# A 1-core attention-and-convolution kernel: x transposed by the DMA crossbar instead of TensorE

## The chip, the cores and the metric

The kernel runs on one core of a Trainium2 chip. The metric is device time in microseconds (us), the median of several executions. Each profile is one execution. Its span is about 1.8 us shorter than that execution's time (931.7 against 933.56 for the kernel before).

Ratios are the mean time of one kernel's fast runs over that of the other's fast runs of the same rounds, with a 95% interval. They are not quite the ratios of the medians quoted beside them.

In the profile lines PE is TensorE, PEld its weight loads, DVE VectorE, ACT ScalarE, POOL GpSimd and SP the engine of the sync queue; a q behind the name is the engine's sequencer, which also issues DMAs. L955 is line 955 of that kernel, x970 a count, `a<-b` an output and what it is made from, ps the memory that TensorE writes its results to. In a costs line the numbers are busy us, mean ns of one, and idle us just before, with what ended most of it. In a line in order of time the bracket is the idle time before it and what ended it.

## The reference, cut to what matters

```python
x = A_q                                          # [1, 2048, 640] bf16
g = sigmoid((x * gate_w).sum(-1, keepdims=True))
a = A_ref(x, A_k, A_v, ...)                      # shifted k times v, long convolution by FFT, times x
b = B_ref(x, wq, wk, wv, wo)                     # attention, 32 heads of 20, one shared k and v head
return g * a + (1 - g) * b
```

x is needed in two layouts: transposed (the 640 columns on partitions) as an operand of the q, k, v and gate projections at the start, and as it is for the gating near the end.

## The kernel before

The program builds a graph of operations and deals them to the engines with a list scheduler of its own. The scheduler walks a model clock, using a cost written at each operation, and fixes every engine's order before the kernel is built. When it finds TensorE under-used it inserts filler matmuls on zeros, to keep TensorE's clock up. A changed cost anywhere can therefore deal the whole attention anew. I call one such order a "deal", and the time before the first exponential the "head".

```python
def loads(self):
    ...
    self.dma(T["gw5"][:, :], ..., writes=["gw5"], nbytes=2000, prio=-6.5)
    self.dma(T["wqst"][:, :, 0:160], wq[:, :, 0:160], ..., prio=-5.5)
    for b in range(NB):                       # 4 blocks of 512 rows
        xl = self.dma(T["xn"][:, 4*b:4*b+4, :], x[:, 4*b:4*b+4, :], writes=[("xn", b)], nbytes=655360, prio=-8 + b)

def xT(self):
    for b in range(NB):
        for dc in range(NDC):                 # 5 column blocks of 128
            gr = self.group("xT", ...)
            for ci in range(4):
                self.mm(gr, lambda e, bk, ...: e.transpose(self.bank_bf(bk, 128, 128*ci), T["xn"][...], T["ident"][:, :]), ...)
            al = self.copy_alts(out, lambda bk: self.bank_bf(bk, 512), True)     # VectorE or ScalarE, as dealt
            self.evac(gr, "dve", None, (), [("xT", b)], 0.45, alts=al)
...                                           # then: query projection, key projection of block 0, key/value
...                                           # projection (kvn), largest key norm, key projections of blocks 1 to 3
def EXP(u, h):
    op("act", lambda e, ...: e.activation(T[f"ET{slot}"][:, :], self.ps[...], ACT.Exp, scale=SCALE), ..., 0.91, name="exp", ...)
...
sch.filler0 = lambda e: e.matmul(self.bank(6)..., self.T["zeros"][:, :], idn, start=True, stop=True)   # fillers of the head
```

## Time and profile before

| what | value |
|---|---|
| time, median | 933.17 us (3 runs), 933.53 with the run beside the changed kernel |
| ScalarE busy | 908.2 us, 97% of the span |
| first exponential starts | 27.67 us |
| from there to the end | 904.0 us |
| idle of ScalarE ahead of the later exponentials | 3.9 us in 7 waits |
| TensorE busy, mean granted clock | 86%, 0.985 |

The page is read from its chain, which is nearly all exponentials on ScalarE. The question is then what precedes the first one and what holds up the others. The prediction shows the lines for both.

### The profile page before, as it was taken

How to read it: one execution, taken by the hardware profiler on the slowest of the kernel's cores; microseconds unless marked ns; L12 is line 12 of the kernel's file. 1: busy time of each engine (PE TensorE's matmuls, PEld its weight loads, DVE VectorE, ACT ScalarE, POOL GpSimd, SP SyncE). 2: the span in 40 equal slices, each digit the busy share in tenths (PEclk: the TensorE clock that was granted, in tenths of full speed). 3: DMA queues.
4: the chain of work that ended last, by engine and by line, in shares of the span. 5: the costliest groups of instructions: out<-in, count | busy, mean ns of one | idle time of the engine just before them, and what ended most of it. 6: DMA issues, size and time to landing. Idle time of an engine off the chain costs nothing.

```text
span 931.7 us, 16366 instructions
## 1 busy us (share of the span) xinstructions
PE 798.1 (86%) x6849; PEld 336.6 (36%) x6913; DVE 617.1 (66%) x816; ACT 908.2 (97%) x1003; POOL 385.8 (41%) x331
## 2 busy tenths in 40 slices
PE   7777778988899888999988899889998889987885
PEld 4222213433444334443332344334443424332132
DVE  7666884466775876676677586567667666566364
ACT  7899999999999999999999999999999999999996
POOL 2870002787423368344285253668354860000000
PEclk9999999999999999999999999999999989999799
DMA  5422632001000001000000100000000012111000
GB/s 158 170 76 79 204 121 64 13 7 40 19 19 19 19 2 41 19 18 19 19 28 16 54 19 18 16 16 7 19 18 19 13 36 74 56 50 42 13 13 29
DMA packets 32631, 39.23 MB, mean 42 GB/s; under 512 B 12371, under 2 KB 25805, under 8 KB 32557
## 3 DMA queue, kind: packets, MB, share of 16 engines
q1 hardware_dynamic: 30957, 37.80, 12.8%
q8 instruction: 54, 0.88, 0.4%
q10 hardware_dynamic: 1600, 0.38, 0.2%
q14 instruction: 20, 0.16, 0.1%
HBM read 31.76 MB, written 6.02 MB: 41 GB/s over the span
## 4 chain that ended last, share of the span: by engine, by line
ACT 94%; PE 5%; DVE 0%; issue 0%; DVEq 0%; POOL 0%; POOLq 0%
ACT ET L955 93%; PE ps L939 1%; PE ps L1387 1%; PE ps L981 1%; ACT xT L545 1%; PE ps L1237 0%; PE ps L1391 0%; PE ps L825 0%; PE ps L839 0%; PE ps L1099 0%; ACT Tsin L734 0%; ACT Tcos L737 0%; DVE outsb L1121 0%; PE ps L1106 0%; ACT L741 0%
## 5 line engine op out<-in xcount | busy, mean ns | idle before, releaser
L955 ACT ACTIVATE ET<-ps 128x1024 bf16<-128x1024 f32 x970 | 890.7, 1196 | 7.0 <-PE ps L939 6.7
L939 PE MATMUL ps<-qT,kT 21*128 21x512 bf16 x2048 | 225.0, 389 | 109.6 <-ACT ET L955 101.4
L1268 POOL TENSOR_TENSOR Pp<-X,K 128x512 f32<-128x512 bf16 x120 | 163.7, 1390 | 269.2 <-DVE K L1256 269.1
L981 PE MATMUL ps<-ET,vaug 128*32 128x512 bf16 x1940 | 209.6, 394 | 1.0 <-ACT ET L955 1.0
L939 PEld LDWEIGHTS ps<-qT,kT 21*128 21x128 bf16 x2048 | 56.2, 91 | 275.4 <-ACT ET L955 266.5
L981 PEld LDWEIGHTS ps<-ET,vaug 128*32 128x32 bf16 x1940 | 52.3, 93 | 117.8 <-issue 113.9
L969 DVE TENSOR_SCALAR dJ<-ps 128x1024 uint32<-128x1024 f32 x54 | 66.0, 1222 | 40.1 <-PE ps L939 39.6
L1268 POOL TENSOR_TENSOR AB<-Pp 128x256 bf16<-128x256 f32 x80 | 82.9, 1036 | 6.1
L974 DVE SCALAR_TENSOR_TENSOR dE<-dJ,dE 128x1024 f32<-128x1024 uint16 x54 | 78.2, 1447 | 0.5
L1301 PE MATMUL ps<-AB,Tcos 128*128 128x256 bf16 x320 | 76.0, 275 | 0.8 <-DVE K L1256 0.7
L977 DVE SCALAR_TENSOR_TENSOR ETd<-dJ,dE 128x1024 bf16<-128x1024 f32 x54 | 75.4, 1397 | 0.8
L976 DVE SCALAR_TENSOR_TENSOR dJ<-dJ 128x1024 f32<-128x1024 uint16 x54 | 73.4, 1359 | 0.7
L1301 PE MATMUL ps<-AB,Tsin 128*128 128x256 bf16 x280 | 67.4, 274 | 0.0
L1387 PE MATMUL ps<-Tcos,zeros 128*128 128x512 bf16 x181 | 60.4, 409 | 5.5 <-issue 5.4
L1268 POOL TENSOR_TENSOR Pp<-Pp 128x512 f32<-128x512 f32 x40 | 59.4, 1486 | 3.1
L1039 DVE COPY acc<-ps 128x512 f32<-128x512 f32 x31 | 21.4, 691 | 49.7 <-PE ps L981 49.3
L1237 PE MATMUL ps<-kv,Tcos 128*128 128x256 bf16 x320 | 47.7, 278 | 1.4 <-DVE K L1256 1.0
L1248 DVE TENSOR_SCALAR X<-ps 128x512 bf16<-128x512 f32 x35 | 24.2, 690 | 37.0 <-PE ps L1237 36.5
L1254 DVE CAST K<-ps 128x256 bf16<-128x256 f32 x40 | 16.9, 423 | 47.5 <-PE ps L1237 47.4
L1237 PE MATMUL ps<-kv,Tsin 128*128 128x256 bf16 x320 | 48.2, 275 | 0.0
L1237 PE MATMUL ps<-ssm_kT,Tsin 128*128 128x256 bf16 x320 | 47.8, 274 | 0.0
L1237 PE MATMUL ps<-ssm_kT,Tcos 128*128 128x256 bf16 x320 | 46.0, 275 | 1.0 <-DVE X L1248 0.5
(137 smaller groups left out, 785.6 us busy)
## 6 DMA issues: line engine op xcount, KB each, us to landing
kslab<-in_A_k_dram SPq DMA_DIRECT2D x15, 640.0 KB, 3.4
rbc<-scr_d SPq DMA_DIRECT2D x31, 256.0 KB
scr_o<-oTn SPq DMA_DIRECT2D x24, 128.0 KB, 1.7
xn<-in_A_q_dram SPq DMA_DIRECT2D x4, 640.0 KB
vslab<-in_A_v_dram SPq DMA_DIRECT2D x16, 160.0 KB, 2.9
kst<-in_A_ssm_k_dram SPq DMA_DIRECT2D x5, 512.0 KB
out_dram<-outsb SPq DMA_DIRECT2D x14, 160.0 KB, 1.8
oTp<-scr_o SPq DMA_DIRECT2D x12, 160.0 KB
```

The costliest lines, as they stand in the source:

```text
L939: o = op("pe", lambda e, r=r, Iu=Iu, g=g, j=j, bk=banks[r]: e.matmul(self.bank(bk), T["kT4"][32 * r:32 * r + 21, 128 * j:128 * j + 128], T ...
L955: op("act", lambda e, p=p, slot=slot: e.activation(T[f"ET{slot}"][:, :], self.ps[:, 1024 * p:1024 * p + 1024], ACT.Exp, scale=SCALE), [("p ...
L969: V(lambda e, p=p: e.tensor_scalar(J[:, :], self.ps[:, 1024 * p:1024 * p + 1024], SCALE * LOG2E * 65536.0, EOFF * 65536.0, ALU.mult, ALU.add),
L974: V(lambda e: e.scalar_tensor_tensor(Ef, lo, ED, Ef, ALU.add, ALU.mult), [kJ, "dE"], ["dE"], c_ps(1024), **k)
L976: V(lambda e: e.scalar_tensor_tensor(Jf, lo, EP, lo, ALU.add, ALU.mult), [kJ], [kJ], c_ps(1024), **k)
L977: V(lambda e: e.scalar_tensor_tensor(T["ETd"][:, :], Jf, EQ, Ef, ALU.add, ALU.mult), [kJ, "dE"], ["ETd"], c_ps(1024), **k)
L981: return op("pe", lambda e, r=r, j=j, src=src: e.matmul(self.bank(6)[32 * r:32 * r + 32, :], T["vaug"][:, j, :], src[:, 512 * (r % 2):512 ...
L1237: o = self.mm(gr, lambda e, bk, lhs=lhs, rhs=rhs, comp=comp, n=n: e.matmul(self.bank(bk, 256, 256 * comp), lhs, rhs, start=(n == 0), stop= ...
L1248: self.evac(gr, "dve", lambda e, bk, parts=parts: e.tensor_scalar(X[:, :, :, :].rearrange("p i a c -> p a i c"), self.bank(bk).rearrange(" ...
L1268: f = lambda e: e.tensor_tensor(out, a, b, alu)
L1301: self.mm(gr, lambda e, bk, lhs=lhs, fc=fc, comp=comp, h=h: e.matmul(self.bank(bk, 256, 256 * h), lhs, AB[:, fc, :, comp, :], start=(fc == ...
L1387: sch.filler = lambda e: e.matmul(self.bank(6), self.T["zeros"][:, :], self.T["Tcos"][:, 0, 0:512], start=False, stop=False)
```

## The change

The intent is to take the transposes off TensorE and their evacuations off ScalarE and VectorE: the DMA writes x already transposed. The plain x is loaded after the first query row, since only the gating reads it. The two small weight loads move to ScalarE's DMA queue, which leaves the sync queue to the transposes.

```diff
-                 nbytes=50000, eng="act", prio=-99)          # wk, wv
+                 nbytes=50000, eng="act", prio=-98.8)        # and -98.7
-        self.dma(T["gw5"]..., prio=-6.5)
-        self.dma(T["wqst"][:, :, 0:160], ..., prio=-5.5)
+        self.dma(T["gw5"]..., eng="act", prio=-98.5)
+        self.dma(T["wqst"][:, :, 0:160], ..., eng="act", prio=-98.9)
         for b in range(NB):
-            xl = self.dma(T["xn"][:, 4 * b:4 * b + 4, :], x[...], writes=[("xn", b)], nbytes=655360, prio=-8 + b)
+            o = T["xT"][:, :, 512 * b:512 * b + 512]
+            i = aps["A_q"][0][512 * b:512 * b + 512, :]
+            xl = self.g.add("sp", lambda e, o=o, i=i: e.dma_start_transpose(o, i), (), [("xT", b)], 0.1, kind="d",
+                            nbytes=1000000, prio=-8 + b)
...
-    def xT(self):                                            # the whole function goes
+    def load_x(self):
+        for b in range(NB):
+            self.dma(T["xn"][:, 4 * b:4 * b + 4, :], x[...], writes=[("xn", b)], nbytes=655360,
+                     prio=30 + b, name="ld_x", after=self.crow0)
...
-                [("ps", 2 * p), ("ps", 2 * p + 1)], [("ET", slot)], 0.91, name="exp", main=True,
+                [("ps", 2 * p), ("ps", 2 * p + 1)], [("ET", slot)], 0.904, name="exp", main=True,
```

The last hunk is not about x: it changes the scheduled cost of an exponential.

More of the change, by code (lines that the diff above doesn't have):

```diff
@@ L656, in loads @@
         self.dma(T["wkv"][:, :, 0:20], aps["B_wk"].rearrange("(dc p) c -> p dc c", p=128), writes=["wk"],
-                 nbytes=50000, eng="act", prio=-99)
+                 nbytes=50000, eng="act", prio=-98.8)
         self.dma(T["wkv"][:, :, 20:40], aps["B_wv"].rearrange("(dc p) c -> p dc c", p=128), writes=["wv"],
-                 nbytes=50000, eng="act", prio=-99)
+                 nbytes=50000, eng="act", prio=-98.7)
         wq = aps["B_wq"].rearrange("(dc p) n -> p dc n", p=128)
         self.dma(T["gw5"][:, :], aps["gate_w"].rearrange("(dc p) -> dc p", p=128), writes=["gw5"], nbytes=2000,
-                 prio=-6.5)
-        self.dma(T["wqst"][:, :, 0:160], wq[:, :, 0:160], writes=[("wqst", 0)], nbytes=204800, prio=-5.5)
+                 eng="act", prio=-98.5)
+        self.dma(T["wqst"][:, :, 0:160], wq[:, :, 0:160], writes=[("wqst", 0)], nbytes=204800, eng="act", prio=-98.9)
         xl = None
         for b in range(NB):
-            xl = self.dma(T["xn"][:, 4 * b:4 * b + 4, :], x[:, 4 * b:4 * b + 4, :], writes=[("xn", b)], nbytes=655360,
-                          prio=-8 + b)
+            o = T["xT"][:, :, 512 * b:512 * b + 512]
+            i = aps["A_q"][0][512 * b:512 * b + 512, :]
+            xl = self.g.add("sp", lambda e, o=o, i=i: e.dma_start_transpose(o, i), (), [("xT", b)], 0.1, kind="d",
+                            nbytes=1000000, prio=-8 + b)
         self.xl = [xl]
@@ L797, in weights2 @@
                       [("wqst", 1)], [("wq_pad", 1)], 1.5, prio=-4, name="wq_cp")
-    def xT(self):
+    def load_x(self):
         T = self.T
+        x = self.aps["A_q"][0].rearrange("(i p) d -> p i d", p=128)
         for b in range(NB):
-            for dc in range(NDC):
-                gr = self.group("xT", 1.0 + 0.1 * b, banks=(0, 1, 2, 3, 4, 5, 7))
-                for ci in range(4):
-                    i = 4 * b + ci
-                    self.mm(gr, lambda e, bk, i=i, dc=dc, ci=ci: e.transpose(
-                        self.bank_bf(bk, 128, 128 * ci), T["xn"][:, i, 128 * dc:128 * dc + 128], T["ident"][:, :]),
-                        [("xn", b), "ident"], 0.1)
-                out = T["xT"][:, dc, 512 * b:512 * b + 512]
-                al = self.copy_alts(out, lambda bk: self.bank_bf(bk, 512), True)
-                self.evac(gr, "dve", None, (), [("xT", b)], 0.45, alts=al)
+            self.dma(T["xn"][:, 4 * b:4 * b + 4, :], x[:, 4 * b:4 * b + 4, :], writes=[("xn", b)], nbytes=655360,
+                     prio=30 + b, name="ld_x", after=self.crow0)
     def kproj(self):
@@ L1361, in build @@
         self.weights()
-        self.xT()
         self.kproj()
@@ L1369, in build @@
         self.tables2()
+        self.load_x()
         self.g.fence(["kslab", "vslab", "w4", "kprod", "kshs"], ["iota_f", "iota_s", "tprod", "tcosp"])
```

## The prediction

> **What bounds the kernel now.** I read the page's chain that ended last first, then the chain in order of time, then the order-of-time view of ScalarE and TensorE in the first 28 us, then the waits of ScalarE. The chain by line:
>
> ```profile
> ACT 94%; PE 5%; DVE 0%; issue 0%; DVEq 0%; POOL 0%; POOLq 0%
> L955 ACT ACTIVATE ET<-ps 128x1024 bf16<-128x1024 f32 x970 | 890.7, 1196 | 7.0 <-PE ps L939 6.7
> ```
>
> The reader is to see that ScalarE carries 94% of the end-setting path, nearly all of it the 970 exponentials of the attention, and that it sat idle ahead of them for only 7.0 us. The change touches none of the 970. What it can move is what lies before the first of them. The same path in order of time, first microseconds:
>
> ```profile
> 2.97 3.59 PE ps L1391 x8
> 6.56 0.93 PE ps L806 x12
> ...
> 8.23 0.97 ACT xT L545 x2
> ...
> 16.22 0.61 ACT xT L545
> ...
> 18.60 0.66 PE ps L839 x20
> 19.26 0.53 PE ps L897 x2
> 19.79 2.16 PE ps L839 x60
> ...
> 23.14 3.19 PE ps L825 x14
> 26.33 0.89 issue
> 27.22 0.45 PE ps L939 x4
> 27.67 75.26 ACT ET L955 x82
> ```
>
> (Columns: start us, length us, what.) The first exponential starts at 27.67 us. Before it the path runs through the x transposes on TensorE (L806), their evacuations on ScalarE (xT, L545), the key/value projection (L839), the key-norm maximum and the key projection (L825). After it, the tail of the kernel: the last exponential ends at 922.6 and 9.1 us of output projection and store follow; the change leaves those as they are. So the head of 27.67 us, 3% of the span, is the whole stake, and 2% of 933.17 is 18.7 us, two thirds of that head.
>
> The tile view of xT gives the evacuations:
>
> ```profile
> L545 ACT ACTIVATE xT<-ps x14: 587/597/627, 7.0 to 19.9; 128x512 bf16<-128x512 bf16 x14
> L544 DVE COPY xT<-ps x6: 415/424/425, 11.9 to 18.1; 128x512 bf16<-128x512 bf16 x6
> ```
>
> (Durations are min/median/max ns, then first and last start.) The last x block is usable only when the evacuations near 20 us have ended, although x itself had landed long before: the stretches of 2 us show 214, 345, 306, 321 and 245 GB/s from 2 to 12 us, together 2.86 MB, which is x (2.62 MB) and the small weights; then 40 GB/s. x was on chip at about 11.5 us. The 8 us between are the price of the TensorE path.
>
> **What the Trainium skill says.** "VectorE: DVE Perf Modes", section "The three transpose paths", gives 128x128 bf16 as 390 ns on TensorE and 1309 ns by the DMA crossbar. The trace has a TensorE transpose at a median of 219 ns, but 24 of them fill 1.79 us, 75 ns each when pipelined; so the page's figure is a latency, and I take its 1309 ns with the same doubt. "Advanced Engine Details and Errata", section "X-Bar Transpose (TRN2)", calls transposing DMAs as fast as regular ones, 350 to 400 GB/s; "DMA: Bandwidth & Descriptors", section "Latency and other measured facts", gives 261 GB/s for one kernel with a non-contiguous middle dimension, and this case writes such a layout (five column blocks of a row go to five places of a partition). No run of the kernel before shows a transposing DMA. The same section of the Advanced page wants no second transpose stream in flight; here all four come from one queue.
>
> **The change, part by part.**
>
> *Removed:* 80 transposes, 80 x 75 ns = 6.0 us of TensorE; 14 evacuations on ScalarE (chained starts about 0.48 to 0.61 us apart, some 7.5 us) and 6 on VectorE (6 x 0.42 = 2.5 us). Of these ScalarE's are on the path, interleaved with eight sine tables that stay.
>
> *Added:* four transposing DMAs of 655 KB on the sync queue, 2.62 MB. At 261 GB/s that is 10.0 us, and with the start of about 2 us that the plain loads show (issue at 0.73, flow from about 2) the last block would land at about 13 us with the small loads beside it. The program's author counts each as 1,000,000 bytes in place of 655,360, a belief in about two thirds of the plain rate; applied to the 320 GB/s that the plain loads show, this is 209 GB/s, 12.5 us, landing at about 15. I choose 16 us as my central estimate of the last landing, a little later, as any work per tile on the issuing side can only add.
>
> *Moved:* the first query weights and the gate weights go to ScalarE's queue: two more issues of about 0.5 us ahead of its table load. These are before its first sine, which VectorE's products hold back anyway; ScalarE then has some 10 us of slack. The later load of x as it is (2.62 MB) follows the first key slabs after 27 us, when the DMA engines have room (page: 2 to 6 tenths busy in the 23 us slices up to 160 us), and is used only from the convolution on. I count nothing for it.
>
> *New order on TensorE* (the built kernel's instruction order shows it): 18 filler matmuls, 10 query-projection, 6 filler, 5 key projection, 6 filler, 2 norms, one gate transpose, 80 key/value, 6 filler, then the maximum and 15 key projections as before. Fillers are fixed work in program order, so TensorE has a floor that no fast DMA goes under: start 2.97; the first 8 fillers 3.59 (as before), 10 more at the 0.216 us spacing that the projections show = 2.2, so 8.7; 10 query 2.2, so 10.9; 6 fillers 1.3, 12.2; 5 key 1.1, 13.3; 6 fillers 1.3, 14.6; norms 0.5, gate transpose and its copy about 0.5, 15.6; 80 key/value 2.2, so **17.8 us**. In the kernel before, this point (end of L839) is at 21.95. From there to the first exponential the order is unchanged and took 27.67 - 21.95 = 5.7 us. So the first exponential comes at about 23.5, 4.2 us earlier, if the last block lands before about 17.2 (its own 20 key/value matmuls need 0.6 us). For each us that it lands later, the exponential is a us later; break-even is a landing at 21.3 us.
>
> *The attention:* the scheduled cost of an exponential is changed from 0.91 to 0.904, which reshuffles fillers and side work. Idle of ScalarE in that stage was 3.9 us in 7 waits (the waits of ScalarE after 30 us), so it can give at most about 4 us back; a reshuffle can also cost 1 or 2. I count zero, with a spread of 2.
>
> Sum: -4.2 with a landing at 16 us. I shade it to -4 because a late first block can leave TensorE idle and start it below its pace: 933.17 - 4.2 = about **929.0 us**.
>
> **Rivals.**
>
> *The DMA becomes the new wait.* If a transposing transfer runs well below the plain one, the last landing, not TensorE's order, sets the head. At 136 GB/s (2.62 MB over 19.3 us) it lands at 21.3 and the change is worth nothing; at 100 GB/s it lands at about 28 and costs 7 us, 940; at the 1309 ns per tile of the skill's table taken as serial, 80 tiles take 105 us and the first exponential is at some 113 us, an end near 1018. For it: a row's block of 128 columns is 256 bytes, so x falls into 10,240 such pieces, far smaller than the 1,280-byte rows of the plain load. Against it: two pages with figures of 261 and more, and the queue's order, which puts nothing ahead of the four transfers.
>
> *ScalarE or VectorE holds the head anyway.* The eight sines and two table loads stay on ScalarE, the 16 table products on VectorE. For it: in the kernel before ScalarE is busy without a gap from 7.5 to 21.5. Against: the gap-free stretch holds 7.5 us of the copies that go; what stays would end near 13 us, before TensorE's 17.8. Were it to bind, the gain would shrink to 1 or 2 us: 931.5.
>
> *Hidden anyway / given back later.* The head shortens by 4 us, but the exponentials are then held by something whose time is not tied to the head, such as the slower start of k and v loads behind the added load of x. Against: the ScalarE queue has only 3.9 us of idle over 895 us, so nothing but the exponentials' own length paces it. It would make 931 to 934.
>
> **Range and chances.** Central case (landing by 17 us, weight 0.55): 926.5 to 931. Landing between 17 and 21 (0.2): 929 to 933. Between 21 and 30 (0.15): 933 to 942. Later (0.1): above 942, and about 0.06 above the 951.8 that is 2% slower. Faster by 2% would need the first exponential at 9 us, which TensorE's fillers and projections alone forbid. I choose 923.5 to 937 as the range: it leaves about 0.05 below (a lucky reshuffle added) and 0.15 above.
>
> **What would show it.** In the changed kernel: no matmul of line L806's kind and no evacuation into xT; the four transposes landing at about 16 us and DMA throughput of 200 GB/s or more up to there; the end of the key/value matmuls near 17.8 us; the first exponential near 23.5; the idle ahead of the exponentials and their mean unchanged; and the time from the first exponential to the end still about 904 us. The prediction is wrong if the key/value matmuls wait for the transpose (the first or the last block), or if the part after the first exponential moves by more than 2 us.

## The result, and the profile after

The changed kernel took 928.96 us (median of 4, 928.4 to 931.0) against 933.53 us. The ratio is 0.9957, interval [0.9934, 0.998]: about 4 us, within 2%. The chain and the exponentials of the changed kernel:

```profile
ACT 93%; PE 5%; DVE 0%; issue 0%; DVEq 0%; POOL 0%; POOLq 0%
L950 ACT ACTIVATE ET<-ps 128x1024 bf16<-128x1024 f32 x970 | 890.6, 1198 | 5.7 <-PE ps L934 5.1
```

The 970 exponentials take the same busy time, 890.6 against 890.7 us, so the bound is the same. The chain of the head in order of time (start us, length us, what):

```profile
2.96 5.47 PE ps L1386 x18
8.43 2.16 PE ps L876 x10
10.59 1.29 PE ps L1386 x6
11.89 1.08 PE ps L820 x5
12.97 1.29 PE ps L1386 x6
14.26 0.58 PE ps L892 x2
...
14.87 0.68 DVE ci L898
15.55 0.10 DVE wkv L815
...
15.69 0.89 PE ps L834 x29
...
17.48 0.67 PE ps L834 x20
18.15 1.30 PE ps L1386 x6
...
23.87 0.45 PE ps L934 x4
24.33 21.18 ACT ET L950 x23
```

There is no evacuation of x left, and no DMA in this chain: it is TensorE's own program order (fillers, query projection, fillers, key projection, fillers, norms), a short detour over VectorE, then the key/value matmuls. The first exponential comes at 24.33 us in place of 27.67. The sync queue of the changed kernel in order of time:

```profile
0.73 13.20 SPq L668 DMA_TRANSPOSE xT<-in_A_q_dram  x4
16.07 0.42 SPq L511 DMA_DIRECT2D wqst<-in_B_wq_dram  x1
```

The issue at 16.07 waits for the last transpose, so the last block had landed by then. Its 20 key/value matmuls start at 17.48, so the DMA had 1.4 us to spare. The waits of ScalarE after the first exponential, first the kernel before, then the changed one (total us, times, longest):

```profile
ACT ET L955 <- PE ps L939: 3.9, 7, 1.2
```

```profile
ACT ET L950 <- PE ps L934: 2.4, 5, 0.7
```

From the first exponential to the end: 904.0 us before, 902.7 after. So 3.35 us of the profiles' difference lie ahead of the first exponential and 1.35 us behind it. The experiments ask two things: what sets the head now, and whether the 1.35 us belong to the change.

### The profile page after: what moved, and what is told of

Read it like the earlier page. It is cut to its first block, busy times and chain, and to the rows that moved or that the text cites. A ratio compares the mean times of both kernels' runs of the same rounds, so it can differ in the third digit from the quotient of the medians.

```text
span 927.0 us, 16240 instructions
## 1 busy us (share of the span) xinstructions
PE 802.8 (87%) x6829; PEld 332.5 (36%) x6829; DVE 607.5 (66%) x810; ACT 901.0 (97%) x989; POOL 377.9 (41%) x331
## 4 chain that ended last, share of the span: by engine, by line
ACT 93%; PE 5%; DVE 0%; issue 0%; DVEq 0%; POOL 0%; POOLq 0%
ACT ET L950 93%; PE ps L1386 1%; PE ps L934 1%; PE ps L1382 1%; PE ps L976 1%; PE ps L820 0%; PE ps L1232 0%; PE ps L1094 0%; PE ps L876 0%; PE ps L1296 0%; PE ps L1178 0%; DVE outsb L1116 0%; PE ps L1101 0%; PE ps L834 0%; DVEq L445 0%
## 5 line engine op out<-in xcount | busy, mean ns | idle before, releaser
L950 ACT ACTIVATE ET<-ps 128x1024 bf16<-128x1024 f32 x970 | 890.6, 1198 | 5.7 <-PE ps L934 5.1
L969 DVE SCALAR_TENSOR_TENSOR dE<-dJ,dE 128x1024 f32<-128x1024 uint16 x54 | 75.5, 1399 | 0.6
L971 DVE SCALAR_TENSOR_TENSOR dJ<-dJ 128x1024 f32<-128x1024 uint16 x54 | 71.2, 1318 | 0.6
L1382 PE MATMUL ps<-Tcos,zeros 128*128 128x512 bf16 x207 | 67.0, 403 | 0.0
L1232 PE MATMUL ps<-ssm_kT,Tsin 128*128 128x256 bf16 x320 | 50.4, 274 | 0.0
L967 DVE TENSOR_SCALAR dE<-dJ 128x1024 uint32<-128x1024 uint32 x54 | 45.6, 845 | 1.4
L876 PE MATMUL ps<-xT,wq_pad 128*128 128x512 bf16 x160 | 44.0, 382 | 1.9 <-DVE qT L544 1.1
```

The costliest lines, as they stand in the source:

```text
L950: op("act", lambda e, p=p, slot=slot: e.activation(T[f"ET{slot}"][:, :], self.ps[:, 1024 * p:1024 * p + 1024], ACT.Exp, scale=SCALE), [("p ...
L967: V(lambda e: e.tensor_scalar(E[:, :], J[:, :], 7, 0x7F800000, ALU.logical_shift_left, ALU.bitwise_and), [kJ], ["dE"], c_fast(1024), **k)
L969: V(lambda e: e.scalar_tensor_tensor(Ef, lo, ED, Ef, ALU.add, ALU.mult), [kJ, "dE"], ["dE"], c_ps(1024), **k)
L971: V(lambda e: e.scalar_tensor_tensor(Jf, lo, EP, lo, ALU.add, ALU.mult), [kJ], [kJ], c_ps(1024), **k)
L1232: o = self.mm(gr, lambda e, bk, lhs=lhs, rhs=rhs, comp=comp, n=n: e.matmul(self.bank(bk, 256, 256 * comp), lhs, rhs, start=(n == 0), stop= ...
L1382: sch.filler = lambda e: e.matmul(self.bank(6), self.T["zeros"][:, :], self.T["Tcos"][:, 0, 0:512], start=False, stop=False)
```

## The experiments

In these tables, "rest" is span minus start of the first exponential, "idle" is ScalarE's later waits for TensorE, both from one profile each.

Together on one chip (kernel before 935.09 us):

| run | first exp. | rest | idle | time | ratio |
|---|---|---|---|---|---|
| after_910 | 25.96 | 908.1 | 7.0 | 933.66 | 0.9976 [0.995, 1.0002] |
| before_904 | 28.13 | 905.6 | 4.6 | 934.02 | 0.9984 [0.9958, 1.001] |
| before_moves | 30.19 | 905.3 | 4.9 | 938.84 | 1.0037 [1.0013, 1.0061] |
| fill_first | 28.23 | 901.9 | 1.4 | 930.19 | 0.9948 [0.9926, 0.9969] |

On another chip (kernel before 935.6 us):

| run | first exp. | rest | idle | time | ratio |
|---|---|---|---|---|---|
| two_more | 30.61 | 903.5 | 2.9 | 935.75 | 1.0005 [0.9986, 1.0023] |
| fill_none | 24.80 | 901.9 | 2.4 | 929.48 | 0.9938 [0.9919, 0.9957] |
| x_beside | 31.98 | 900.7 | 1.4 | 934.22 | 0.9997 [0.9969, 1.0026] |
| after_again | 24.97 | 903.4 | 3.0 | 928.95 | 0.9927 [0.9909, 0.9945] |
| after_910_again | 24.50 | 905.5 | 5.0 | 934.32 | 0.9987 [0.9968, 1.0007] |
| after_907 | 24.57 | 903.1 | 3.2 | 929.96 | 0.9945 [0.993, 0.996] |
| head_mended | 24.53 | 902.7 | 1.6 | 928.72 | 0.9929 [0.9912, 0.9946] |

Rest minus idle lies between 899.3 and 901.1 us in all of them, whatever the head: the rest is, within 2 us, a constant plus what ScalarE waits.

### Two more transposes ahead: does the head count one for one?

```diff
             def tr(e, o=o, i=i, b=b):
+                if b == 0:
+                    for n in range(2):       # into the space of the plain x, overwritten later
+                        e.dma_start_transpose(xo_n, x_block_n).then_inc(self.xsem, 16)
                 return e.dma_start_transpose(o, i)
```

The order of all engines is as in the changed kernel.

> The changed kernel, same schedule, with two more transposing transfers of the same size ahead of the four (into space that is overwritten later). Theory (1.4 us of slack behind the landing at 16.07, after that one us late for one us; each transfer takes the 3.29 us of its issue): landing at about 22.6, first exponential at 22.6 + 0.6 + 0.5 + 5.7 = 29.4 us, so 5 us later than in the changed kernel and 934 us, ratio 1.001. Rival (the landing is hidden by other work of the head, as in a head bound by the tables or the fillers): first exponential 24.3 to 26 us, 929 to 931.

The first exponential came at 30.61 us, 5.6 us after that of after_again, and the time rose by 6.8 us on the same chip with the same deal. So the head counts at about one for one here; the rest is unchanged (903.5 against 903.4). In x_beside, below, it counts for less: 7.0 us later and 5.3 us slower than after_again. The road was not the one expected. All blocks had landed by 21.3 us, before TensorE's order reached the key/value matmuls at 21.99. It had waited for the first block instead:

```profile
12.95 3.95 PE L886 MATMUL ps<-xT,wq_pad 128*128 128x512 bf16 x10 [4.42 <-DMA xT<-in_A_q_dram]
```

The ten query projections stood idle 4.42 us for the first block and then took 3.95 us in place of 2.32, because TensorE's clock had fallen meanwhile (granted clock 0.50 from 14 to 16 us). In an in-order program an early first block can matter more than an early last one.

### Fillers taken out: is TensorE's order the bound?

```diff
+        drop = set(o for r in runs[1:] for o in r)      # fill_none: all runs of the head; fill_first: all but the first
+        sch.order["pe"] = [o for o in pe if o not in drop]
```

> The changed kernel, same schedule, with three of the four runs of filler matmuls in the head taken out (6 each; the first 18 stay). Theory (the head is now TensorE's own order, with the transposes' landing at 16.07 us 1.4 us behind it): the key/value matmuls catch up with the last transposed block, the last key square starts at 17.2 in place of 18.62, the first exponential comes at about 22.9 in place of 24.3, and the time falls by about 1.4 us, ratio 0.994. Rival 1 (the landing of the transposes already sets the head): nothing moves, 24.3. Rival 2 (TensorE runs slower without the fillers): matmuls of 128x512 take more than the 0.216 us spacing and the gain is lost.

> The changed kernel, same schedule, with all fillers of the head taken out. Theory (transposes' landing is the next bound): first exponential at about 22.9 us, as with three of the four runs out; the last transposed block at 16.07 sets it. Rival (fillers hold TensorE at speed): the first ten projections take about 0.45 us each, as the first eight fillers of the kernel before did, and the first exponential is at 23.5 or later.

My theory failed in both: I expected 22.9 us, and got 28.23 and 24.80. In fill_none (order of time on TensorE):

```profile
7.51 4.03 PE L876 MATMUL ps<-xT,wq_pad 128*128 128x512 bf16 x10 [7.51 <-DMA xT<-in_A_q_dram]
11.37 1.24 PE L820 MATMUL ps<-xT,wk 128*128 128x512 bf16 x5
14.72 0.59 PE L892 MATMUL ps<-sq,IndG 128*8 128x512 bf16 x2 [2.11 <-DVE IndG L709]
15.25 0.17 PE L813 MATMUL ps<-ident,gw 5*128 5x5 bf16 x1
16.18 2.46 PE L834 MATMUL ps<-wkv,xT 128*128 128x41 bf16 x80 [0.75 <-DVE wkv L815]
```

The first block lands at 7.51 us, so the projections can start 0.9 us sooner, but at half speed (4.03 us for ten; the clock column does not show this first stretch, the durations do). Then the norms wait 2.11 us for small constant columns that VectorE makes late in its order. The fillers filled waits that exist anyway. The bound of the head is thus the program order of TensorE together with VectorE's small operations, and removing fillers alone gains nothing: 929.48 against 928.95 us.

fill_first shows what a gap can cost. After the same 2.11 us wait the granted clock fell to 0.50 and stayed there up to 26 us (length of the stretch, TensorE busy, clock, DMA share, GB/s):

```profile
14.00:16.00 2.00, 0.56 (x2) 0.94 0.64 144
16.00:18.00 2.00, 1.26 (x30) 0.50 0.44 82
...
24.00:26.00 2.00, 2.00 (x6) 0.50 0.40 108
```

In fill_none the same wait was followed by no fall: its clock is 1.00 in every stretch from 14 to 28 us. So a gap of this length may cost the clock or not, and these runs do not show what decides. In fill_first's profile the first exponential is 3.9 us later than in the first profile of the changed kernel. Yet the median, 930.19, does not lie that far from the kernels with all fillers, so one execution's head is not every execution's.

### The plain x loaded beside the transposes: what holds the transposes?

```diff
+            for b in range(NB):              # on the scalar queue, right after the gate weights
+                e.dma_start(T["xn"][:, 4*b:4*b+4, :], x[:, 4*b:4*b+4, :]).then_inc(self.xsem, 16)
```

> The changed kernel, same schedule, with a second, plain load of x (2.62 MB) issued on the scalar queue at the start, beside the transposes. Theory (the transposes are held by their own issue on the sync queue, 3.29 us each, while the DMA engines are half busy): the four issues still take about 3.3 us each, the last lands at 16 to 18 us. Rival (the transposes are held by the DMA engines): two streams share, issues stretch to 5 us or more and the last lands at 21 us or later, the first exponential at 28 us. In both cases scalar work starts about 2 us later, which has 2.6 us of room.

The rival's forecast of the landing came true. The tile view of xT, first the changed kernel, then this one (min/median/max ns of an issue, first and last start us):

```profile
L668 SPq DMA_TRANSPOSE xT<-in_A_q_dram x4: 3157/3287/3330, 0.7 to 10.6; - x4
```

```profile
L674 SPq DMA_TRANSPOSE xT<-in_A_q_dram x4: 3013/3859/7605, 0.7 to 16.0; - x4
```

One of the four issues stretched to 7.6 us and the last block arrived at about 23.6 us. The first exponential came at 31.98, 4 us later than the rival said: the landing was 2.6 us later than its 21, and TensorE's clock fell to 0.50 while it waited 4.11 us for that block. I had taken a DMA figure near 1.1 in a 2 us stretch for half busy, but it is the mean busy share of all 16 engines. Compare the kernel before (plain loads), the changed one (transposes) and this run (both):

```profile
4.00:6.00 2.00, 2.00 (x6) 0.66 (x5) 2.00 (x7) 0.73 (x1) 0.36 (x2) 1.00 1.13 345
```

```profile
4.00:6.00 2.00, 2.00 (x6) 0.70 (x5) 2.00 (x5) 1.99 (x5) 1.13 (x2) 1.00 1.34 228
```

```profile
12.00:14.00 2.00, 2.00 (x11) 0.87 (x9) 1.64 (x8) 1.98 (x3) 0.00 (x0) 1.00 1.11 371
20.00:22.00 2.00, 0.00 (x0) 0.00 (x0) 0.55 (x3) 0.03 (x1) 0.00 (x0) 0.58 1.20 74
```

(Length of the stretch; busy us of TensorE, its weight loads, VectorE, ScalarE and GpSimd; then clock, DMA share, GB/s.) By this share the engines look full at 228 GB/s with transposes and at 345 GB/s with plain loads. But a full share is no fixed limit of bytes: with both streams they moved 371 GB/s at a share of 1.11, and only 74 at 1.20. So the two streams hold each other up, which my theory excluded; whether it is the engines themselves or something else on the transposing path is not shown. The plain x is better loaded after the transposes than beside them, where it costs the whole gain (ratio 0.9997).

### The weight loads alone

```diff
-        self.dma(T["gw5"]..., prio=-6.5)
+        self.dma(T["gw5"]..., eng="act", prio=-98.5)       # and the first query weights, in the kernel before
```

> The kernel before with only the first query weights and the gate weights moved to the scalar queue, ahead of x. Theory (the evacuations of the transposes hold the head, not the weights): first exponential within 1 us of 27.7 us, ratio 0.999 to 1.001. Rival (the weights' wait of 3.1 us on GpSimd was the head's limit and most of the gain comes from the move): first exponential near 25 us, ratio 0.997.

It was slower than both theories allowed: first exponential at 30.19 us, ratio 1.0037. GpSimd copied the query weights at 6.24 us in place of 10.33 (it still waited 2.68 us for them, in place of 3.09), but four issues on ScalarE's queue delayed its table load, from 1.87 to 4.47 us. The first evacuation of x starts only 0.25 us later, at 7.27 us, yet the one that the query projections wait for starts at 13.38 in place of 11.87: the head was dealt anew as well, and how much of this the table load causes is not shown. TensorE's query projections began at 14.04 in place of 12.78 us and ran at half speed (granted clock 0.53 from 14 to 16 us), 634 ns a matmul in the median in place of 379:

```profile
6.24 0.85 POOL L786 COPY wq_pad<-wqst 128x800 bf16<-128x800 bf16 x1 [2.68 <-DMA wqst<-in_B_wq_dram]
14.04 4.02 PE L881 MATMUL ps<-xT,wq_pad 128*128 128x512 bf16 x10 [0.77 <-ACT xT L545]
```

The moved loads are no gain by themselves. Whether they help in the order without evacuations was not tested: no run has the changed kernel without them.

### The scheduled cost of an exponential

```diff
-        0.904, name="exp"      # after_910, after_907: the changed kernel with 0.91 or 0.907
-        0.91, name="exp"       # before_904: the kernel before with 0.904
```

> The changed kernel with the scheduled cost of an exponential put back from 0.904 to 0.91; the instruction order of the head is the same, that of the attention is dealt anew. Theory (the gain is the earlier first exponential, 3.35 us in the profiles; the 1.35 us gained after it is an accident of the deal): first exponential at 24.3 us, and 0 to 2 us slower than the changed kernel, so 929 to 931. Rival (the new cost is a real part of the gain): the stretch after the first exponential is back at 904 us and the ratio to the kernel before is nearer 1, about 0.9965 in place of 0.9957.

> The kernel before with only the scheduled cost of an exponential changed to 0.904. Theory (accident of the deal): ratio to the kernel before between 0.998 and 1.002, with no fixed sign, first exponential at 27.7 us. Rival (the cost is worth 1.3 us by itself): ratio 0.9985, and the idle ahead of the exponentials falls from 3.9 to about 2.4 us.

> The changed kernel with the scheduled cost at 0.91, second time. If the deal of the attention is worth something: slower than the changed kernel of the same call by 1.5 to 4 us, with idle ahead of the exponentials again near 7 us in place of 2 to 3. If the earlier 7.0 was one execution's accident (dips of the granted clock): the same time as the changed kernel within 1 us, idle between 2 and 5 us.

> The changed kernel with the scheduled cost at 0.907, half way: a third deal with the same head. If the time followed the cost, it would lie between 0.904 and 0.91. If it is an accident of each deal, it lies anywhere within 4 us of either, with its idle as the measure: time minus that of the changed kernel equals the difference of the two idle sums.

> The changed kernel again, unaltered, for a comparison with the two next runs on one chip. Ratio to the kernel before 0.9957 within its interval; first exponential between 24.3 and 26.0 us by the length of TensorE's half-speed start (5.5 to 6.9 us for the first 18 fillers in the profiles so far); idle ahead of the exponentials after the first 2 to 3 us.

My theory of after_910 (929 to 931 us) failed: it took 933.66 us. With one chip and the same head in program order, 0.904, 0.907 and 0.91 gave 928.95, 929.96 and 934.32 us. The changed kernel without its new cost is only 0.1 to 0.2% faster than the kernel before (ratios 0.9976 and 0.9987, 1 within both intervals). The kernel before with the new cost is not clearly faster (0.9984, interval around 1), and its idle rose from 3.9 to 4.6 us. So the cost isn't worth something by itself: it picks a deal, and the deals of the changed kernel differ by up to 5 us. The idle of one profile does not account for that by itself: after_910_again idles 2.0 us more than after_again and its median is 5.4 us longer, and after_907 idles 0.2 more and is 1.0 longer. The profiled execution of after_910_again, 932.95, was one of its faster ones.

What a deal does is seen at 867 to 873 us. First the kernel before, then the changed one with 0.91 (from 870), then the changed one (columns as above):

```profile
867.00:870.00 3.00, 2.01 (x11) 0.43 (x11) 1.92 (x3) 2.77 (x4) 0.00 (x0) 0.52 0.03 3
870.00:873.00 3.00, 2.53 (x15) 0.66 (x15) 2.96 (x4) 2.09 (x3) 0.00 (x0) 0.50 0.03 3
```

```profile
870.00:873.00 3.00, 3.00 (x16) 0.53 (x12) 2.43 (x4) 2.47 (x3) 0.00 (x0) 0.50 0.03 3
```

```profile
867.00:870.00 3.00, 2.22 (x15) 0.50 (x11) 2.93 (x5) 3.00 (x5) 0.00 (x0) 1.00 0.18 56
870.00:873.00 3.00, 2.42 (x21) 0.64 (x21) 1.84 (x2) 3.00 (x5) 0.00 (x0) 1.00 0.16 56
```

In the first two TensorE's clock has fallen to one half and ScalarE waits for scores (2.09 and 2.47 busy of 3). In the third neither happens. Both profiles with 0.91 in the changed kernel, and both of the kernel before, have waits near 763 and 870 us; both profiles of the changed kernel have waits near 772 and 779 and none near 870. The places recur with the deal. One place does not make a deal slow: after_907 falls at 863 us too and is nearly as fast as after_again. Others, such as one near 487 us in the kernel before, appear in one execution and not in the next.

> The kernel before again, unaltered, for a second profile of it. Theory (the changed kernel gains from an earlier first exponential and from a deal with fewer falls of TensorE's clock): first exponential at 27.7 to 28.2 us, the stretch after it 904 to 907 us, idle ahead of the exponentials 4 to 7 us with waits again near 526, 760 and 870 us. Rival (the first profile's 3.9 us was typical and the clock falls are random): idle 2 to 4 us at other places. Ratio to itself 1.000 within its interval.

The kernel before a second time: 934.81 us, ratio to itself 0.9995 [0.9954, 1.0036]; first exponential at 28.46, rest 903.7, idle 3.8, with waits near 527, 763 and 871 us. That is the theory for the places, and the rival for the sum. Two profiles each then give means of 28.06 and 24.65 us for the first exponential, 3.4 us apart, and of 903.9 and 903.05 for the rest, 0.85 apart.

The clock on record lets head and deal be told apart in the timed executions too, not only in the profiles. Each of them comes with its mean granted clock. At a recorded clock of 0.985 or 0.986 there are five executions of the kernel before, 932.7 us in the mean, and seven of the changed head in its three deals, 929.9: 2.8 us less. A straight-line fit over all 58 executions of these kernels that have a clock on record (one slope, one constant for the kernel before and one for the changed head) gives 2.9 us, with a 95% interval of 2.5 to 3.3, and 4.2 us for each 0.01 of the clock; with a constant for each deal, the three deals lie within 0.5 us of each other. What the deals differ in is the clock: a mean of 0.989 with 0.904, 0.985 with 0.907, 0.978 with 0.91, and 0.981 in the kernel before. So the earlier head is worth about 3 us, and the deal with 0.904 about 3 more than that of the kernel before. This is a correlation, read after the runs, and no run set the clock on purpose.

### A mended head

```diff
+        drop = set(runs[2])                                       # the third run of 6 fillers
+        move([o for o in dve if o in self.small], q0)             # constant columns before the first query evacuation
+        move([gwt_ev], q2_ev)                                     # the gate column before the norms' evacuation
```

> The changed kernel, same deal, with TensorE kept busy but its detours cut: the third run of 6 fillers is dropped, the small constant columns that the norm matmul waits for are made earlier on VectorE, and the gate column's copy is taken ahead of the norm's evacuation. Theory (TensorE's order was the bound, the landing of the transposes near 16 us is next): the 80 key/value matmuls start at about 14 us, the last 20 wait for the landing, last key square at 17.2, first exponential at 22.9 us, 1.4 us earlier than in the changed kernel; time 0.9 to 1.5 us lower, ratio 0.994. Rival: a new gap lets TensorE's clock fall to half, as with the fillers taken out, and the first exponential comes at 24.3 or later.

The time was 928.72 us against 928.95: no gain shown, where 0.9 to 1.5 us were expected. This execution's first 18 fillers took 6.78 us in place of 5.47, which alone is 1.3 us, and the gate column still waited:

```profile
2.97 6.78 PE L1388 MATMUL ps<-ident,zeros 128*128 128x512 bf16 x18 [2.97 <-DVE ident L690]
...
15.22 0.16 PE L815 MATMUL ps<-ident,gw 5*128 5x5 bf16 x1 [0.41 <-DVE IndG L710]
15.91 2.46 PE L836 MATMUL ps<-wkv,xT 128*128 128x41 bf16 x80 [0.53 <-DVE wkv L817]
```

The key/value matmuls started at 15.91, not at 14. Constant columns of a later stage and a key evacuation stood ahead of the gate's copy on VectorE. No version clearly beats the changed kernel.

## Why the prediction was right

- **The stake** was named right: the exponentials' busy time is unchanged (890.7 and 890.6 us), and two_more shows that the head counts at about one for one.
- **The landing** of the last block was estimated at 16 us and measured at 16.07, in other profiles 15.5 to 15.7. That it fits so well is partly luck. The rate was taken as 209 GB/s for the whole. In fill_none blocks two to four (1.97 MB) came in the 8.0 us from 7.51 to 15.51, 246 GB/s, and the first took 6.8 us from its issue, where 209 GB/s from 2 us on would have had it there at 5.1 us. The stream began later and ran faster than assumed, and the two misses offset. It also did not hold 200 GB/s throughout, as forecast: three of the seven stretches from 2 to 16 us show 164, 141 and 188.
- **TensorE's floor** was the binding step, as predicted, with the DMA 1.4 us behind it. Its size was off by 0.8 us: the last key square is at 18.62 where 17.8 was worked out. The terms up to the norms came 0.3 us better than worked out; two others were mis-sized. The gate transpose and its copy took 0.85 us, not 0.5, because VectorE's copy stands behind the norms' evacuation. And the 80 key/value matmuls took 2.93 us up to the release of the last key square, not 2.2: the 21.95 of the kernel before, with which I compared, already held 0.5 us of that release. From there to the first exponential it was 5.70 us in both kernels, as predicted. So the first exponential came at 24.33 where 23.5 was said.
- **"Fillers are fixed work"** gave the right bound for the wrong reason. Without them the head is no shorter (fill_none), since waits for VectorE and a slower clock take their place.
- **ScalarE as rival**: its second table load ended at 13.72 us where about 13 was worked out, before TensorE's floor. It did not bind. Two readings behind this were off: ScalarE's stretch without a gap ends at 20.84 us and not at 21.5, and its first sine was not held back by VectorE; it ran at once after the table load, at 3.27 us, and moved to 4.47 with the two added issues. The slack absorbed it.
- **The attention** was counted at zero with a spread of 2 us. In the two profiles each it gave 0.85 us in the mean; by the fit over executions the deal is worth about 3 us. This is the term whose spread was mis-sized: with the cost at 0.91 the same change is 5.4 us slower on one chip. By its own sign of being wrong (more than 2 us after the first exponential) the prediction passes in the profiles, with 1.35, and would not by the fit. It fell within 0.1 us of the median because the head gave 0.8 us less than said and the deal gave about as much more: that is luck. Its sum also says that it shades 4.2 to 4 and then subtracts 4.2.
- **The later load of x** cost nothing visible: the changed kernel's first wait of ScalarE after the start is at 118 us, though x itself moved from 26 us on, when the DMA engines carried up to 408 GB/s, other loads included.

How much of the gain is the head cannot be read from one profile: the first 18 fillers took 5.47 to 6.87 us in the profiles that have them, by the length of the half-speed start. The two profiles each put the head at 3.4 us, the executions at an equal clock at 2.8 to 2.9. On the second chip the gain was 6.7 us in the medians, and there the mean clock was 0.989 against 0.981: by the fit, 3.4 us of it are the deal. What stays open is which property of an order lets TensorE's clock fall less often.

## What to carry to other kernels

Work taken off three engines is worth only what it lets the one critical engine start earlier; here 80 transposes and 20 evacuations bought about 3 us of 930, because the head then ran into its own program order. Where an automatic scheduler deals the rest anew, compare several deals before crediting the change: the deals here differ by more than the change gains. And a filler is removed safely only together with the wait that it covers, since an idle TensorE can come back at half speed: it did after 4.42 us in two_more and after 2.11 us in fill_first, and did not after the same 2.11 us in fill_none.

## What the Trainium skill lacked or had wrong

- "Advanced Engine Details and Errata", section "X-Bar Transpose (TRN2)", has transposing DMAs as fast as regular ones, 350 to 400 GB/s. Here, in this five-block layout, they ran at 228 to 248 GB/s in the 2 us stretches with a DMA share of 1 or more, small weight loads included, against 345 for the plain load. The lower of the two figures that the prediction cites is the nearer one.
- "VectorE: DVE Perf Modes", section "The three transpose paths", gives 1309 ns for 128x128 by the crossbar with no word whether that is a latency or a rate. Pipelined, 60 such tiles took 8.0 us, 133 ns each; TensorE's took 75 ns each where the table has 390. Neither figure of the table can be used as a rate.
- "TensorE: Matmul & The Clock Gate", section "Part 1: The HAM clock gate (the "warmup" mystery)", describes the fall to half clock after an idle window and says that the start-up is run-variable. The second agrees: 5.47 to 6.87 us for the first 18 fillers. The section also tells of falls from frequent short pauses between groups of matmuls, without saying how much idling is enough. Here, in the kernel before, the clock was at 0.52 in the stretch from 867 to 870 us, after three stretches of 3 us in each of which TensorE was about two thirds busy (1.94 to 2.18 us) with gaps of up to 0.58 us, and one of 1.11 us at the fall.
- No page says for this chip how long a transposing DMA of this size from device memory holds its issuing queue: one issue of 655 KB occupied the sync queue for 3.16 to 3.33 us, and up to 7.6 us beside a plain load, where a plain load of the same size took about 0.4 to 1.2 us at the start of the kernel before.
